# Attention with two MoE layers on one core: plain fp32 scores of two heads side by side

## The chip, the cores and the metric

The kernel runs on one core of one Trainium2 chip. The metric is the device time of one execution in microseconds (us). The engines are named as in the profile: PE is TensorE (PEld its weight loads), DVE VectorE, ACT ScalarE, POOL GpSimd, SP the queue that issues the DMAs.

## The reference

Attention over 4 batches and 8 heads (S = 576, D = 64) with a memory term, then two gated MoE layers on 2304 tokens; all in fp32:

```python
def _attn_ref(q, k, v, M_prev, z_prev, beta):
    scores = scale * np.matmul(q, k.transpose(0, 1, 3, 2))
    scores = np.where(causal, -1000000000.0, scores)
    a = np.exp(scores - scores.max(-1, keepdims=True))
    a /= a.sum(-1, keepdims=True) + 1e-09
    local = np.matmul(a, v)
    q_p = phi(q)                      # where(x > 0, x, exp(x) - 1) + 1
    mem_out = (q_p @ M_prev) / ((q_p @ z_prev)[..., None] + 1e-06)
    g = 1.0 / (1.0 + np.exp(-beta))
    return g * mem_out + (1 - g) * local
# x = attention output, (2304, 512); d_ff = 1536
x = (sigmoid(x @ w_gate) * (x @ w_val)) @ w_out
x = ((x @ w_a) * (x @ w_b)) @ w_out2
```

## The kernel before

Attention runs over 16 pairs of heads (`p`), four to a batch. The 576 rows of a head lie in five blocks of queries, the first of 64 rows, the others of 128, so that block `i` sees 128 i + 64 keys (64, 192, 320, 448, 576: 1600 key columns a head). The blocks are worked in two sets, `X_` = 0, 2, 3 and `Y_` = 1, 4.

For a pair, `load_rows` brings queries and keys in. `cut_q` cuts the queries into a rounded part (VectorE) and the rest (GpSimd), both of type fp32r; the keys are loaded twice. `turn` and `turn4` transpose them on TensorE into PSUM tiles `tp`, five blocks for each head and for each of the two; `put` scales the queries on VectorE, rounds the keys on ScalarE and takes the rest on VectorE. The 128 rows of a turned tile are the two parts of one head. `scores` multiplies: two fp32r products for a block and head, against the rounded keys and against the rest. `expo` adds the mask and takes the row extreme on VectorE (line 244), then the exponential on ScalarE. `turn_w` transposes the weights in three groups (A, B, C) and `evac` copies them to SBUF, all on ScalarE (`EDVE` is empty). `phi1` and `phi2` make the memory term, `sums` the denominators; `turn_mix` and `turn_r` transpose them. `pv` multiplies with the values: plain fp32 products, head 0 in output partitions 0 to 63 and head 1 in 64 to 127. `pv` of set X_ comes one iteration after its pair, that of Y_ at the start of the second iteration after.

Into this the first MoE layer is woven for three of the batches (`moe_a`): 48 steps a batch, each of three fp32r products of 512 columns (`mm3`, lines 490 to 492), four steps to a group that adds up in one PSUM bank. `Ms()` places one step (twelve of them in an iteration); a batch's steps begin when its four pairs are finished. At a group's end the bank is read by `gcopy` (VectorE), by `gat`, which goes through `gate` (line 568, VectorE), or by `fin`. `fill` places pieces of the preparation of the MoE weights (`w_stream`), on VectorE, ScalarE, GpSimd and by DMA. After the last pair the second stage begins with the products of `gv`.

PSUM has eight banks: two for `sc`, two for `sd` (both for scores; for the first four pairs alone, then `psm`, two banks for the MoE groups, has their place), four for `tp`. Instructions are written in the order of the iteration; a planner with a model of the times sets the order on each engine and holds an instruction back where its buffer isn't free.

Of the kernel before, what the change touches and what calls it, by code (L numbers as in the profile page):

```python
# [19 lines left out]
def kernel(  # L20
# [17 lines left out]
    P = 128  # L38
# [30 lines left out]
    pst = rctx.enter_context(tc.tile_pool(name="pst", bufs=4, space=bass.MemoryType.PSUM))  # L69
    pctx = ExitStack()  # L70
    psc = pctx.enter_context(
        tc.tile_pool(name="psc", bufs=1, space=bass.MemoryType.PSUM, side="right")
# [15 lines left out]
    ident_r = at.tile([P, P], F32R, name="ident_r", bufs=1)  # L88
    scs = [psa.tile([P, 1024], F32, tag="sc", name="sc"), psc.tile([P, 1024], F32, tag="sd", name="sd")]
# [67 lines left out]
    def cut_q(p):  # L157

        t = at.tile([P, NB, 2, 2, D], F32R, tag="qc", name="qc", bufs=1)
        vec.tensor_copy(out=t[:, :, :, 0], in_=st["qn", p])  # L160
        pool.tensor_tensor(
            out=t[:, :, :, 1], in0=st["qn", p], in1=t[:, :, :, 0].bitcast(F32), op=ALU.subtract
        )
        st["qc", p] = t

    def put(p, e, key, src, a, z):
        if key == "q":
            if a == 0:
                st["q", p, e] = at.tile([P, S], F32R, tag="qt", name="qt")
            vec.tensor_scalar(  # L170
                out=st["q", p, e][:, a:z], in0=src, scalar1=-1.0 / D ** 0.5, scalar2=None,
                op0=ALU.mult,
            )
            return
        if a == 0:
            st["k", p, e] = [at.tile([P, S], F32R, tag=x, name=x) for x in ("kh", "kl")]
        kh, kl = st["k", p, e]
        act.activation(out=kh[:, a:z], in_=src, func=AF.Copy)
        vec.tensor_tensor(
            out=kl[:, a:z], in0=src, in1=kh[:, a:z].bitcast(F32), op=ALU.subtract  # L180
        )

    def turn1(out, p, e, key, i):
        if key == "q":
            pe.transpose(
                out=out.bitcast(F32R), in_=st["qc", p][:, i, e].rearrange("p r d -> p (r d)"),
                identity=ident_r,
            )
        else:
            pe.transpose(  # L190
                out=out, in_=st["kn", p][:, i, e].rearrange("p r d -> p (r d)"), identity=ident
            )

    def turn(p, e, key):
        t = tp()
        for i, c in C03.items():
            turn1(t[:, c:c + P], p, e, key, i)
        put(p, e, key, t[:, 0:CUT], 0, CUT)

    def turn4(p, e):  # L200
        t = tp()
        for c, key in enumerate("kq"):
            turn1(t[:, c * P:(c + 1) * P], p, e, key, 4)
        for c, key in enumerate("kq"):
            put(p, e, key, t[:, c * P:(c + 1) * P], CUT, S)

    def sc_of(p, blocks):

        return scs[blocks is Y_ and p < NPAIR]

    def scores(p, e, blocks):
        sc = sc_of(p, blocks)
        qs, ks = st["q", p, e], st["k", p, e]
# [16 lines left out]
    def expo(p, e, blocks):  # L230
        if blocks is X_:
            st["mx", p, e] = at.tile([P, NB], F32, tag="mx", name="mx")
        sc = sc_of(p, blocks)
# [275 lines left out]
    def moe_a(b):  # L509
# [31 lines left out]
        def outp(u, c, f):  # L541
            if c == 0 and f == 0:
                mo[:] = [bank() for _ in H2]
            o = (2 * u + f) * P
            mm3(mo[f], ws[0, c, 2], slice(o, o + P), *gs[c], c == 0, c == MA - 1)

        def fin(u):
            io = pairs()
            vec.tensor_copy(out=io[:, 0], in_=mo[0])
            act.activation(out=io[:, 1], in_=mo[1], func=AF.Copy)  # L550
            nc.sync.dma_start(out=x2d[b][:, 2 * u:2 * u + 2], in_=io)
# [8 lines left out]
        for u in H2:  # L560
            for c in range(MA):
                for f in H2:
                    last = f and c == MA - 1
                    yield b, (0, c, 2), partial(outp, u, c, f), partial(fin, u) if last else None
# [14 lines left out]
    def start():  # L579
        make_identity(nc, ident)  # L580
        act.activation(out=ident_r, in_=ident, func=AF.Copy)
# [143 lines left out]
    EDVE = ""  # L725
    if True:
# [82 lines left out]
        cut_q(0)  # L809
        for e in H2:  # L810
            turn(0, e, "k")
            turn(0, e, "q")
            turn4(0, e)
        for p in range(NP + 2):
            new = p < NP
            nx = p + 1 if p + 1 < NP else None
            old = p - 1 if 0 < p <= NP else None
            last = p - 2 if p >= 2 else None
            if p == NPAIR:
                pctx.close()  # L820
                mctx = ExitStack()
                psm = mctx.enter_context(
                    tc.tile_pool(name="psm", bufs=2, space=bass.MemoryType.PSUM, side="right")
                )
# [4 lines left out]
            if new:  # L829
                scores(p, 0, X_)  # L830
                expo(p, 0, X_)
            Ms()
            if last is not None:
                pv(last, Y_)
            Ms()
            if old is not None:
                turn_w(old, 1, "B")
                turn_w(old, 1, "C")
            Ms()
            fill(p)  # L840

            if new:
                scores(p, 0, Y_)
                expo(p, 0, Y_)
            if old is not None:
                sums(old)
            Ms()
            if new:
# [3 lines left out]
                turn_w(p, 0, "A")  # L852
            if nx:
                cut_q(nx)
# [3 lines left out]
            if new:  # L858
                scores(p, 1, X_)
                expo(p, 1, X_)  # L860
            if nx:
                load_z(nx)
            Ms()
            if nx:
                turn(nx, 0, "k")
                turn(nx, 0, "q")
            Ms()
            if new:
                turn_w(p, 0, "B")
                turn_w(p, 0, "C")  # L870
            if nx:
                turn4(nx, 0)
            Ms()
            if old is not None:
                for name in "01Y":
                    turn_mix(old, name)
            fill(p)

            if new:
                scores(p, 1, Y_)  # L880
                expo(p, 1, Y_)
                phi2(p)
            Ms()
# [6 lines left out]
            if nx:  # L890
                turn(nx, 1, "k")
                turn(nx, 1, "q")
                turn4(nx, 1)
            if new:
                turn_w(p, 1, "A")
            Ms()
# [104 lines left out]
```

## Time and profile before

| | |
|---|---|
| median of 3 runs | 1172.28 us (1172.09 to 1174.34) |
| profiled execution | 1174.15 us, its span 1172.3 us |
| busy share of the span | PE 97%, PEld 80%, DVE 48%, ACT 41%, POOL 29% |
| attention with the woven first layer | to 359.37 us of the span |
| DMA | 89.67 MB, mean 76 GB/s |

Busy time of PE is the union of records whose ends are modelled, so a full PE can still hold short pauses. A plain fp32 product is two records on PE, an fp32r product or a transposition is one. A line can be that of a helper: 151 is every copy through `rnd`, 490 to 492 every `mm3`.

### The profile page before, as it was taken

To read this page: it belongs to the slowest core of one execution; us is meant where nothing else is said; L and a number is where in the kernel's file an instruction comes from. 1 tells how busy PE (TensorE), PEld (TensorE's weight loads), DVE (VectorE), ACT (ScalarE), POOL (GpSimd) and SP (SyncE) were. 2 spreads that over 40 slices of the span, in tenths; PEclk is the share of its full clock that TensorE was granted. 3 is DMA by queue.
4 is the path that set the end of the run, shared out by engine and by line. 5 is a ranking of instruction groups with operands and counts; after the bars stand their busy time and mean duration, and the time that the engine had idled before them with its cause. 6 is when DMAs were issued, how large, how long until landed. Compare 5 with 4: busy or idle time off the path is not lost.

```text
span 1172.3 us, 16189 instructions
## 1 busy us (share of the span) xinstructions
PE 1136.2 (97%) x6088; PEld 932.6 (80%) x6088; DVE 563.3 (48%) x1233; ACT 479.8 (41%) x1042; POOL 340.5 (29%) x330
## 2 busy tenths in 40 slices
PE   6889889999999999999999999999999999999998
PEld 5667678788777778998888888878888888888897
DVE  6898978565545995137621587851100200200111
ACT  5978767867853444134312234422111211211221
POOL 5786777463420112111111111111111111111111
PEclk9989989999999999999999999999999999999999
DMA  7454446243112443024420345311000200100010
GB/s 174 111 148 108 129 104 172 58 95 114 48 50 89 134 126 107 34 64 134 126 90 18 109 125 160 110 54 36 37 1 1 72 1 1 59 1 1 5 37 18
DMA packets 130814, 89.67 MB, mean 76 GB/s; under 512 B 90416, under 2 KB 118064, under 8 KB 129840
## 3 DMA queue, kind: packets, MB, share of 16 engines
q1 hardware_dynamic: 130736, 88.63, 26.2%
q8 instruction: 48, 0.79, 0.3%
q14 instruction: 30, 0.25, 0.1%
HBM read 71.31 MB, written 17.30 MB: 76 GB/s over the span
## 4 chain that ended last, share of the span: by engine, by line
PE 59%; DVE 5%; DMA 3%; issue 1%; POOL 0%; ACT 0%; POOLq 0%; DVEq 0%; ACTq 0%
PE gv L492 13%; PE gv L491 13%; PE gv L490 13%; PE mo L687 4%; PE mo L686 4%; PE mo L685 4%; PE mo L491 3%; PE mo L492 3%; PE mo L490 3%; DMA st<-in_moe_w_gate_dram 2%; DMA st<-in_moe_w_out_dram 1%; DVE w L459 1%; DVE wl L446 1%; DVE wt L417 1%; DVE st L456 1%; DVE wl L420 1%
## 5 line engine op out<-in xcount | busy, mean ns | idle before, releaser
L574 POOL TENSOR_TENSOR gl<-sg,gh 128x512 fp32r<-128x512 f32 (+1 forms) x120 | 143.6, 1197 | 698.0 <-ACT gh L151 670.9
L492 PE MATMUL gv<-xs,w 128*128 128x512 f32 (+1 forms) x864 | 318.3, 368 | 0.0
L490 PE MATMUL gv<-xs,w 128*128 128x512 f32 (+1 forms) x864 | 318.3, 368 | 0.0
L491 PE MATMUL gv<-xs,w 128*128 128x512 f32 (+1 forms) x864 | 318.2, 368 | 0.0
L568 DVE TENSOR_TENSOR sg<-gv,sg 128x512 f32<-128x512 f32 (+1 forms) x108 | 68.0, 630 | 417.6 <-PE gv L492 413.0
L490 PEld LDWEIGHTS gv<-xs,w 128*128 128x128 f32 x864 | 162.7, 188 | 29.5
L491 PEld LDWEIGHTS gv<-xs,w 128*128 128x128 f32 x864 | 162.8, 188 | 29.4
L492 PEld LDWEIGHTS gv<-xs,w 128*128 128x128 f32 x864 | 162.7, 188 | 28.7
L151 ACT ACTIVATE gh<-sg 128x512 fp32r<-128x512 f32 (+1 forms) x120 | 70.6, 588 | 208.8 <-DVE sg L568 208.5
L655 ACT ACTIVATE sg<-gv 128x512 f32<-128x512 f32 (+1 forms) x108 | 59.0, 547 | 220.6 <-PE gv L492 216.7
L249 ACT ACTIVATE s<-s,mx 128x320 f32<-128x320 f32 (+3 forms) x128 | 78.0, 611 | 25.2 <-DVE mx L244 24.4
L687 PE MATMUL mo<-w,gl 128*128 128x512 f32 x216 | 85.1, 394 | 0.6 <-POOL gl L574 0.5
L686 PE MATMUL mo<-w,gh 128*128 128x512 f32 x216 | 84.8, 393 | 0.0
L685 PE MATMUL mo<-w,gh 128*128 128x512 f32 x216 | 84.8, 392 | 0.0
L151 ACT ACTIVATE aw<-tp 128x512 f32<-128x512 f32 (+1 forms) x144 | 70.6, 508 | 27.7 <-PE tp L330 21.4
L418 ACT ACTIVATE wt<-wt,rebias 128x512 int32<-128x512 int32 x72 | 51.6, 721 | 66.1 <-DVE wt L417 66.0
L491 PE MATMUL mo<-gl,w 128*128 128x512 f32 (+1 forms) x192 | 70.9, 369 | 3.8 <-POOL gl L574 3.6
L244 DVE CUSTOM_DVE_ANT_0 s<-sc,mask 64x64 f32<-64x64 f32 (+4 forms) x144 | 62.2, 470 | 19.9 <-PE sc L219 19.8
L490 PE MATMUL mo<-gh,w 128*128 128x512 f32 (+1 forms) x192 | 70.4, 366 | 0.0
L492 PE MATMUL mo<-gh,w 128*128 128x512 f32 (+1 forms) x192 | 70.2, 366 | 0.0
L219 PE MATMUL sc<-kh,qt 128*64 128x64 f32 (+1 forms) x168 | 54.1, 344 | 4.4 <-ACT s L249 1.9
L455 ACT ACTIVATE w<-wt 128x512 fp32r<-128x512 f32 x57 | 36.1, 633 | 48.2 <-DVE wt L452 48.0
(111 smaller groups left out, 1840.4 us busy)
## 6 DMA issues: line engine op xcount, KB each, us to landing
st<-in_moe_w_out_dram SPq DMA_DIRECT2D x24, 512.0 KB, 3.5
kn<-in_k_dram SPq DMA_DIRECT2D x64, 128.0 KB, 2.8
st<-in_moe_w_gate_dram SPq DMA_DIRECT2D x12, 512.0 KB, 4.2
st<-in_moe_w_val_dram SPq DMA_DIRECT2D x12, 512.0 KB, 3.6
st<-in_moe_w_a_dram SPq DMA_DIRECT2D x12, 512.0 KB, 3.6
st<-in_moe_w_b_dram SPq DMA_DIRECT2D x12, 512.0 KB, 3.7
xd<-x SPq DMA_DIRECT2D x16, 288.0 KB, 2.7
qn<-in_q_dram SPq DMA_DIRECT2D x32, 128.0 KB, 2.7
```

The lines of the kernel that those rows point to most:

```text
L151: act.activation(out=out, in_=src, func=AF.Copy)
L244: st["pace"] = vec.tensor_tensor_reduce(out=s, in0=sc[0:m, SC0[i]:SC0[i] + w], in1=mask[0:m, c:c + w], scale=1.0, scalar=BIG, op0=ALU.add, ...
L249: act.activation(out=o, in_=s, func=AF.Exp, scale=-1.0, bias=mx[0:m, i:i + 1], accum_out=sm[0:m, i:i + 1],)
L490: pe.matmul(o, lhsT=w[:, 0, ws_], rhs=xh, start=first, stop=False, skip_group_check=True)
L491: pe.matmul(o, lhsT=w[:, 0, ws_], rhs=xl, start=False, stop=False, skip_group_check=True)
L492: pe.matmul(o, lhsT=w[:, 1, ws_], rhs=xh, start=False, stop=last, skip_group_check=True)
L568: st["gate"] = vec.tensor_tensor(out=s[:, 0:n], in0=vps[:, 0:n], in1=s[:, 0:n], op=ALU.mult)
L574: pool.tensor_tensor(out=gl[:, 0:n], in0=s[:, 0:n], in1=gh[:, 0:n].bitcast(F32), op=ALU.subtract)
L655: act.activation(out=s[:, 0:n], in_=tg[:, 0:n], func=AF.Copy if layer else AF.Sigmoid)
L685: pe.matmul(mo[f], lhsT=gh[:, t], rhs=w[:, 0], start=first, stop=False)
L686: pe.matmul(mo[f], lhsT=gh[:, t], rhs=w[:, 1], start=False, stop=False)
L687: pe.matmul(mo[f], lhsT=gl[:, t], rhs=w[:, 0], start=False, stop=c == NCH - 1)
```

## The change

Queries and keys are turned uncut, both heads in one tile: the 128 rows of a turned tile are head 0 (0 to 63) and head 1 (64 to 127). So a pair has ten turns in place of twenty, and `cut_q`, the second load of the keys and the split of the turned keys go. The scores are plain fp32 products over 64 rows, for a block first head 0 and then head 1, each into its own two banks `sc0` and `sc1`. An iteration has two score phases (X_ and Y_, both heads) and not four. `pv` of Y_ follows `pv` of X_ in the iteration after the pair; the loop has 17 iterations, before 18. The MoE steps stay twelve in an iteration, at other places. PSUM: four banks for scores, three for `tp`, one for MoE groups; the output products of a MoE batch go one bank after the other. The minimum in `phi1` moves from GpSimd to VectorE, the evacuation of group C from ScalarE to VectorE. Buffers of the exponentials go from two to three, those of the groups B and C from three to two.

```diff
-    pst = rctx.enter_context(tc.tile_pool(name="pst", bufs=4, space=bass.MemoryType.PSUM))
+    pst = rctx.enter_context(tc.tile_pool(name="pst", bufs=3, space=bass.MemoryType.PSUM))
+    psm = mctx.enter_context(
+        tc.tile_pool(name="psm", bufs=1, space=bass.MemoryType.PSUM, side="right")
...
-    scs = [psa.tile([P, 1024], F32, tag="sc", name="sc"), psc.tile([P, 1024], F32, tag="sd", name="sd")]
+    scs = [psa.tile([P, 1024], F32, tag=f"sc{e}", name="sc") for e in H2]
...
-        st["kn", p] = at.tile([P, NB, 2, 2, D], F32, tag="kn", name="kn", bufs=1)
-        for r in H2:
-            load_rows(st["kn", p][:, :, :, r], k, p)
+        st["kn", p] = at.tile([P, NB, 2, D], F32, tag="kn", name="kn", bufs=2)
+        load_rows(st["kn", p], k, p)
...
-    def cut_q(p):
...
+    def put(p, key, src, a, z):
+        if a == 0:
+            st[key, p] = at.tile([P, S], F32, tag=f"{key}t", name=f"{key}t")
+        t = st[key, p][:, a:z]
         if key == "q":
             vec.tensor_scalar(
+                out=t, in0=src, scalar1=-1.0 / D ** 0.5, scalar2=None, op0=ALU.mult
             )
         else:
+            act.activation(out=t, in_=src, func=AF.Copy)
+
+    def turn1(out, p, key, i):
+        src = st[f"{key}n", p][:, i].rearrange("p h d -> p (h d)")
+        pe.transpose(out=out, in_=src, identity=ident)
...
+    def scores(p, blocks):
         for i in blocks:
             w, m = width(i), rows(i)
             r0 = max(P * i - 64, 0)
             for a, z in [(0, w)] if i < 4 else [(0, ZX), (ZX, w)]:
-                for s in H2:
+                for e in H2:
+                    r = slice(64 * e, 64 * e + 64)
                     st["anchor"] = pe.matmul(
-                        sc[0:m, SC0[i] + a:SC0[i] + z], lhsT=qs[:, r0:r0 + m], rhs=ks[s][:, a:z],
-                        start=(s == 0), stop=(s == 1),
+                        scs[e][0:m, SC0[i] + a:SC0[i] + z], lhsT=st["q", p][r, r0:r0 + m],
+                        rhs=st["k", p][r, a:z], start=True, stop=True,
                     )
...
-        both = at.tile([P, wa + wb], F32, tag=f"s{blocks[-1]}", name="s")
+        both = at.tile([P, wa + wb], F32, tag=f"s{blocks[-1]}", name="s", bufs=3)
...
-        pool.tensor_scalar(out=e, in0=qn, scalar1=0.0, scalar2=None, op0=ALU.min)
+        vec.tensor_scalar(out=e, in0=qn, scalar1=0.0, scalar2=None, op0=ALU.min)
...
-        st["a", p, e, name] = evac("aw" + name, t, len(NAMES[name]) * P, 3, name in EDVE)
+        st["a", p, e, name] = evac("aw" + name, t, len(NAMES[name]) * P, 3 if name == "A" else 2, name in EDVE)
...
+        def outp(f, c):
+            if c == 0:
+                mo[:] = [bank()]
+            mm3(mo[0], ws[0, c, 2], slice(f * P, f * P + P), *gs[c], c == 0, c == MA - 1)
...
-    EDVE = ""
+    EDVE = "C"
...
+        for p in range(NP + 1):
...
             if new:
+                scores(p, X_)
+                for e in H2:
+                    expo(p, e, X_)
             if old is not None:
+                for e in H2:
+                    turn_w(old, e, "B")
+            Ms()
             if old is not None:
+                for e in H2:
+                    turn_w(old, e, "C")
+                sums(old)
+            Ms(2)
             fill(p)
             if new:
                 phi1(p)
                 if p:
                     load_v(p)
             if nx:
+                load_z(nx)
+                for key in "kq":
+                    turn(nx, key)
             Ms(2)
             fill(p)
             if new:
+                scores(p, Y_)
+                for e in H2:
+                    expo(p, e, Y_)
             Ms()
             if old is not None:
                 for name in "01Y":
                     turn_mix(old, name)
+            Ms()
+            if nx:
+                turn4(nx)
             fill(p)
             if new:
+                for e in H2:
+                    turn_w(p, e, "A")
                 phi2(p)
+            Ms(2)
             if old is not None:
                 room(old)
                 turn_r(old, X_)
                 turn_r(old, Y_)
                 Ms()
                 pv(old, X_)
+                pv(old, Y_)
+            Ms(2)
             fill(p)
```

## Rows read from the trace of the kernel before

**Rows 1.** The page, busy tenths of each engine in 40 slices of the span.

```profile
PE   6889889999999999999999999999999999999998
...
DVE  6898978565545995137621587851100200200111
```

**Rows 2.** Four stretches: length, busy (xcount) of PE, PEld, DVE, ACT, POOL; PEclk, DMA, GB/s.

```profile
0.00:10.84 10.84, 3.56 (x18) 2.89 (x19) 3.77 (x11) 3.79 (x8) 6.54 (x11) 1.00 0.59 132
10.84:159.65 148.81, 129.97 (x907) 103.75 (x907) 132.11 (x364) 118.01 (x316) 110.64 (x109) 0.95 0.52 133
159.65:359.37 199.72, 199.40 (x1351) 159.07 (x1350) 121.49 (x348) 134.89 (x339) 95.34 (x104) 0.99 0.33 86
359.37:450.00 90.63, 86.99 (x374) 69.52 (x373) 78.38 (x134) 40.75 (x64) 13.94 (x10) 1.00 0.42 128
```

**Rows 3.** All engines in order of time, the start: us, length, what [idle before].

```profile
7.05 1.53 POOL L161 TENSOR_TENSOR qc<-qn,qc 128x640 fp32r<-128x640 f32 x1
...
8.63 0.57 PEld L185 LDWEIGHTS tp<-ident_r,qc 128*128 128x128 f32 x4 [0.41 <-POOL qc L161]
```

**Rows 4.** VectorE's groups by line, 10 to 360 us: busy us, mean ns | idle.

```profile
L170 DVE TENSOR_SCALAR qt<-tp 128x448 fp32r<-128x448 f32 x32 | 19.7, 616 | 7.2 <-PE tp L185 7.2
L179 DVE TENSOR_TENSOR kl<-tp,kh 128x448 fp32r<-128x448 f32 x32 | 19.6, 612 | 8.3 <-ACT kh L178 8.1
...
L179 DVE TENSOR_TENSOR kl<-tp,kh 128x128 fp32r<-128x128 f32 x32 | 9.0, 281 | 1.6 <-ACT kh L178 1.5
L160 DVE CAST qc<-qn 128x640 fp32r<-128x640 f32 x15 | 8.9, 593 | 0.0
L170 DVE TENSOR_SCALAR qt<-tp 128x128 fp32r<-128x128 f32 x32 | 8.8, 277 | 0.0
```

**Rows 5.** TensorE in order of time, 200 to 222 us (pairs 8 and 9).

```profile
200.09 0.60 PE L190 MATMUL tp<-ident,kn 128*128 128x128 f32 x4
200.45 0.54 PE L185 MATMUL tp<-ident_r,qc 128*128 128x128 f32 x4
200.82 0.47 PE L490 MATMUL m<-xs,w 128*128 128x512 f32 x1
...
201.71 0.34 PE L219 MATMUL sc<-kh,qt 128*128 128x192 f32 x1
...
202.55 0.40 PE L490 MATMUL m<-xs,w 128*128 128x512 f32 x1
...
204.71 1.65 PE L343 MATMUL tp<-ident,mix 64*128 64x64 f32 x10
206.12 0.27 PE L219 MATMUL sc<-kh,qt 128*64 128x64 f32 x1
...
207.16 0.64 PE L360 MATMUL tp<-ident,rt 64*128 64x64 f32 x3
...
210.85 1.25 PE L385 MATMUL tp<-aw,vn 128*64 128x256 f32 x12
212.04 0.65 PE L190 MATMUL tp<-ident,kn 128*128 128x128 f32 x4
```

**Rows 6.** Line 385, 210.2 to 212.1 us: ns min/median/max, starts, forms.

```profile
L385 PE MATMUL tp<-aw,vn x12: 272/379/379, 210.9 to 211.8; 128*64 128x256 f32 x8, 128*64 128x128 f32 x4
```

**Rows 7.** In order of time, records that begin before 211.0 us.

```profile
210.85 0.39 PE L385 MATMUL tp<-aw,vn 128*64 128x256 f32 x2
```

**Rows 8.** In order of time: ends of two MoE groups (135 to 141, 314 to 317 us).

```profile
135.55 0.39 PE L492 MATMUL m<-xs,w 128*128 128x512 f32 x1
...
139.79 0.68 DVE L568 TENSOR_TENSOR sg<-m,sg 128x512 f32<-128x512 f32 x1
...
314.05 0.39 PE L491 MATMUL m<-xs,w 128*128 128x512 f32 x1
...
314.28 0.39 PE L492 MATMUL m<-xs,w 128*128 128x512 f32 x1
...
314.81 0.69 DVE L568 TENSOR_TENSOR sg<-m,sg 128x512 f32<-128x512 f32 x1
```

More of the change, by code (lines that the diff above doesn't have):

```diff
@@ L68 @@
     psa = rctx.enter_context(tc.tile_pool(name="psa", bufs=1, space=bass.MemoryType.PSUM))
-    pst = rctx.enter_context(tc.tile_pool(name="pst", bufs=4, space=bass.MemoryType.PSUM))
-    pctx = ExitStack()
-    psc = pctx.enter_context(
-        tc.tile_pool(name="psc", bufs=1, space=bass.MemoryType.PSUM, side="right")
+    pst = rctx.enter_context(tc.tile_pool(name="pst", bufs=3, space=bass.MemoryType.PSUM))
+    mctx = ExitStack()
+    psm = mctx.enter_context(
+        tc.tile_pool(name="psm", bufs=1, space=bass.MemoryType.PSUM, side="right")
     )
@@ L87 @@
     rebias = const.tile([P, 1], F32, name="rebias")
-    ident_r = at.tile([P, P], F32R, name="ident_r", bufs=1)
-    scs = [psa.tile([P, 1024], F32, tag="sc", name="sc"), psc.tile([P, 1024], F32, tag="sd", name="sd")]
+    scs = [psa.tile([P, 1024], F32, tag=f"sc{e}", name="sc") for e in H2]
     sms = [at.tile([P, NB, 2], F32, name=f"sm{i}", bufs=1) for i in H2]
@@ L154, in tp @@
         return pst.tile([P, 512], F32, tag="tp", name="tp")
-    def cut_q(p):
[L159 to L166, printed above, removed]
+    def put(p, key, src, a, z):
+        if a == 0:
+            st[key, p] = at.tile([P, S], F32, tag=f"{key}t", name=f"{key}t")
+        t = st[key, p][:, a:z]
@@ L167, in put @@
         if key == "q":
-            if a == 0:
-                st["q", p, e] = at.tile([P, S], F32R, tag="qt", name="qt")
             vec.tensor_scalar(
[L171 to L187, printed above, removed]
-            )
-        else:
-            pe.transpose(
-                out=out, in_=st["kn", p][:, i, e].rearrange("p r d -> p (r d)"), identity=ident
-            )
@@ L194, in turn @@
-    def turn(p, e, key):
+                out=t, in0=src, scalar1=-1.0 / D ** 0.5, scalar2=None, op0=ALU.mult
+            )
+        else:
+            act.activation(out=t, in_=src, func=AF.Copy)
+    def turn1(out, p, key, i):
+        src = st[f"{key}n", p][:, i].rearrange("p h d -> p (h d)")
+        pe.transpose(out=out, in_=src, identity=ident)
+    def turn(p, key):
         t = tp()
         for i, c in C03.items():
-            turn1(t[:, c:c + P], p, e, key, i)
-        put(p, e, key, t[:, 0:CUT], 0, CUT)
@@ L200, in turn4 @@
-    def turn4(p, e):
+            turn1(t[:, c:c + P], p, key, i)
+        put(p, key, t[:, 0:CUT], 0, CUT)
+    def turn4(p):
         t = tp()
         for c, key in enumerate("kq"):
-            turn1(t[:, c * P:(c + 1) * P], p, e, key, 4)
+            turn1(t[:, c * P:(c + 1) * P], p, key, 4)
         for c, key in enumerate("kq"):
[L205 to L213, printed above, removed]
+            put(p, key, t[:, c * P:(c + 1) * P], CUT, S)
@@ L232, in expo @@
             st["mx", p, e] = at.tile([P, NB], F32, tag="mx", name="mx")
-        sc = sc_of(p, blocks)
+        sc = scs[e]
         mx, sm = st["mx", p, e], sms[p % 2][:, :, e]
         wa, wb = width(blocks[-2]), width(blocks[-1])
-        both = at.tile([P, wa + wb], F32, tag=f"s{blocks[-1]}", name="s")
+        both = at.tile([P, wa + wb], F32, tag=f"s{blocks[-1]}", name="s", bufs=3)
         st["w", p, e, blocks[-2]], st["w", p, e, blocks[-1]] = both[:, 0:wa], both[:, wa:wa + wb]
@@ L539, in gat, with fin @@
                 finished.append(b)
[L541 to L551, printed above, removed]
+        def outp(f, c):
+            if c == 0:
+                mo[:] = [bank()]
+            mm3(mo[0], ws[0, c, 2], slice(f * P, f * P + P), *gs[c], c == 0, c == MA - 1)
+        def fin(f):
+            if f % 2 == 0:
+                sg["io"] = pairs()
+            io = sg["io"]
+            if f % 2:
+                act.activation(out=io[:, 1], in_=mo[0], func=AF.Copy)
+                nc.sync.dma_start(out=x2d[b][:, f - 1:f + 1], in_=io)
+            else:
+                vec.tensor_copy(out=io[:, 0], in_=mo[0])
         for kind, then in ((0, gcopy), (1, gat)):
@@ L559, in moe_a @@
                     )
-        for u in H2:
+        for f in range(KD):
             for c in range(MA):
-                for f in H2:
-                    last = f and c == MA - 1
-                    yield b, (0, c, 2), partial(outp, u, c, f), partial(fin, u) if last else None
+                yield (
+                    b, (0, c, 2), partial(outp, f, c), partial(fin, f) if c == MA - 1 else None
+                )
     def gate(vps, s, n, tag="g"):
@@ L580, in start @@
         make_identity(nc, ident)
-        act.activation(out=ident_r, in_=ident, func=AF.Copy)
         vec.memset(rebias, -896.0 * 2 ** 23)
@@ L808 @@
         load_v(0)
[L809 to L814, printed above, removed]
+        for key in "kq":
+            turn(0, key)
+        turn4(0)
+        for p in range(NP + 1):
             new = p < NP
             nx = p + 1 if p + 1 < NP else None
[L817 to L824, printed above, removed]
+            old = p - 1 if p else None
             if nx:
@@ L829 @@
             if new:
[L830 to L834, printed above, removed]
+                scores(p, X_)
+                for e in H2:
+                    expo(p, e, X_)
+            if old is not None:
+                for e in H2:
+                    turn_w(old, e, "B")
             Ms()
             if old is not None:
-                turn_w(old, 1, "B")
-                turn_w(old, 1, "C")
-            Ms()
+                for e in H2:
+                    turn_w(old, e, "C")
+                sums(old)
+            Ms(2)
             fill(p)
[L842 to L847, printed above, removed]
             if new:
@@ L851 @@
                     load_v(p)
-                turn_w(p, 0, "A")
             if nx:
-                cut_q(nx)
+                load_z(nx)
+                for key in "kq":
+                    turn(nx, key)
             Ms(2)
@@ L858 @@
             if new:
[L859 to L872, printed above, removed]
+                scores(p, Y_)
+                for e in H2:
+                    expo(p, e, Y_)
             Ms()
@@ L876 @@
                     turn_mix(old, name)
+            Ms()
+            if nx:
+                turn4(nx)
             fill(p)
             if new:
-                scores(p, 1, Y_)
-                expo(p, 1, Y_)
+                for e in H2:
+                    turn_w(p, e, "A")
                 phi2(p)
-            Ms()
+            Ms(2)
             if old is not None:
@@ L889 @@
                 pv(old, X_)
[L890 to L896, printed above, removed]
+                pv(old, Y_)
+            Ms(2)
             fill(p)
```

## The prediction

> **What bounds the kernel now.** I read the busy slices first, then the time of each engine in four stretches, then the costs by line, then TensorE's queue in order of time. The change touches the attention stage and the first MoE layer that is woven into it, so the end of that stage is the number that matters: the first `gv` product of the next stage follows the last woven product at 359.37 us, and nothing that the later stages do is changed. In the slices, 29.3 us each, VectorE is about as full as TensorE for the first seven and half full for the next six [rows 1]. The stretches [rows 2] make that sharp. From 10.84 to 159.65 us (pairs 0 to 7) VectorE is busy 132.11 of 148.81 us, ScalarE 118 and GpSimd 111, TensorE has gaps: VectorE sets the pace, with two engines close behind. From 159.65 to 359.37 us (pairs 8 to 15 and the tail) TensorE is busy 199.40 of 199.72 us and VectorE 121: here only TensorE counts. Before 10.84 us nothing scores yet. So each part of the change has three prices, one for each stretch.
>
> After 359.37 us the next stage is paced by VectorE (78 of 90.63 us) preparing weights. That work starts when attention has given up its space, so a stage that ends earlier moves the rest earlier, whole.
>
> **The start.** Today a pair needs queries cut into two parts (`cut_q`: VectorE, then 1.53 us on GpSimd) and two copies of the keys. The first query turn waits for GpSimd's cut until 8.63 us [rows 3], and the first scores start at 10.84. After the change there is no cut and half the key loads. I take 2.5 us off: GpSimd's 1.53 us plus some 0.9 us for one head's eight turns less ahead of the first score [rows 5]. Bounds: 0 (if the query load itself is late) and 4 us (both heads ready at once).
>
> **Pairs 0 to 7, VectorE's price.** Removed for each pair [rows 4]: the cast of the queries 0.59 us; four cut-off parts of the keys, 2 x 0.612 + 2 x 0.281 = 1.79 us; one of the two scalings of the queries, 0.616 + 0.277 = 0.89 us. Sum 3.27 us. Added: the minimum over 128x640 that leaves GpSimd; no row has it on VectorE, its bounds are the cast of the same size, 0.59, and the scaling stretched from 448 to 640 columns, 0.88; I take 0.65, near the cast, since both go from SBUF to SBUF. And the two "C" evacuations of 384 columns that leave ScalarE: 0.69 us for 512 from PSUM [rows 8] gives 0.52 each, 1.04. Net -1.58 us a pair, 12.6 us over eight. ScalarE and GpSimd lose more than that each, so neither takes over. What can eat it: the four score phases of a pair become two, so that VectorE has fewer other things in hand while it waits for scores. I take 10 us; bounds 0 (the pace is a chain of waits and not VectorE's load) and 14.
>
> **Pairs 8 to 15, TensorE's price.** The clearest rows are TensorE's queue in order of time [rows 5]. Turns of keys and queries: four and four run from 200.09 to 200.82 us, 0.09 us each; a pair has twenty, of which ten go, 0.9 us. Seven pairs are still turned in this stretch: -6.3 us.
>
> Scores: one head's blocks 1 and 4 run from 201.71 to 202.55 us, its blocks 0, 2 and 3 from 206.12 to 207.16: 1.88 us a head, 3.76 a pair. The new form is a plain fp32 product, and the value products show its price. Each is two records in the trace; a record of 256 columns lasts 0.379 us, one of 128 columns 0.272 [rows 6], so 0.84 ns a column for each. Twelve records with 2560 columns in all would take 2.15 us one after another; they took 1.19 us, from 210.85 to 212.04 [rows 5], and the first two lie on top of each other, 0.39 us for both [rows 7]. So two heads on two halves of the array run at once. There the halves are output columns, in the new scores they are contraction rows; no row shows that kind. If it pairs too, a pair of heads needs 1600 columns x 2 records x 0.84 ns = 2.7 us; if not, 5.4 us. I take pairing, since the value products show two tiles of the array working independently.
>
> To this comes the cost of changing the tile size. Ten turns of `mix`, two of them with 64 rows, take 1.41 us from 204.71 to 206.12 where ten of the full size would take 0.9: 0.5 us for four changes, 0.12 each. The new scores have five changes a pair (into block 0, out of it, out of that phase, in and out of the other), 0.6 us, so 3.3 us a pair and -0.5 against today: -4 us over eight pairs. (The Trainium skill, "TensorEngine Tiling (Array Packing)", section "Key Properties", says that changing the tiling mode drains TensorE. That speaks against this form and agrees with the 0.12 us; had the trace shown no such cost, the saving would be 1.0 us a pair and the sum 4 to 5 us lower.)
>
> Woven MoE steps: twelve a pair before and after, three products of 0.23 us each [rows 8]. A batch of 48 steps can start when its four pairs are finished, which today is after the first quarter of the second iteration behind, and after the change at the end of the one before. So three steps of the first batch move out of this stretch: 9 x 0.23 = -2.1 us.
>
> **What it costs: the banks.** Both heads now hold score space at once. The turns keep three banks of four (they have 16 tiles a pair instead of 19), and the MoE steps one of two. A group of twelve products then has to be evacuated before the next group's first product. In TensorE's stretch the way from the last product's start to the end of its evacuation is 314.28 to 315.50 us, 1.2 us; in VectorE's stretch 135.55 to 140.47, 4.9 us, since the evacuation queues behind other VectorE work [rows 8]. With two banks this hides: TensorE shows no gap. With one, behind the waiting product stand the next pair's scores and turns in TensorE's queue, and behind those VectorE's reductions. The full price is 1.2 - 0.23 = 1.0 us for each of the 24 groups in TensorE's stretch; zero if turns or value products always stand between two groups. There are 11 to 12 us of attention work in each iteration and three groups, so most can be covered; I take a third of the full price, +8 us, bounds 0 and 24. For three instead of four turn banks, and for the last pair's value products which now stand directly ahead of the next stage with little behind them to hide their evacuation, +2 us (0 to 4).
>
> **The sum.** -2.5 - 10 - 6.3 - 4 - 2.1 + 8 + 2 = -14.9 us. The profiled execution took 1174.15 us, 1.85 us over its span of 1172.3 and 1.87 us over the median of the runs, 1172.28; so 1159.3 us by it and about 1157 us by the median.
>
> **Rivals.** (a) *The single MoE bank decides.* The gains come to 24.9 us and the other costs to 2; over all 36 groups the change breaks even when a group costs 0.6 us on average. At the full 1.0 us in TensorE's stretch and about 1 us for each of the twelve in VectorE's, the cost is 36 instead of 8: 1157 + 28 = 1185 us. For it: VectorE's stretch shows evacuations far behind, and TensorE executes its queue in order. Against it: there is other TensorE work to put between.
> (b) *The row halves do not pair.* 5.4 + 0.6 = 6.0 us a pair instead of 3.3, 2.7 x 8 = 22 us more, and some 3 us more in pairs 5 to 7, where TensorE has the woven steps already: 1182 us. That is the case in which the change doesn't do what it says.
> (c) *VectorE's load isn't the pace in pairs 0 to 7.* Its waits there are short, but if the chain from scores to exponentials sets the pace, the 10 us go: 1167 us.
> (d) *Everything hides.* No cost of banks and the upper bounds of the gains: -4 - 14 - 6.3 - 4 - 2.1, 1142 us.
>
> **How the numbers follow.** Forecast 0.55 (1145 to 1166 us), (a) at or past break-even 0.18, (b) 0.10, (c) 0.09, (d) 0.08. The predicted time is the forecast's, 1157 us. The range runs from (d) to just short of (a) and (b), 1141 to 1181 us: it leaves out the worse halves of both and a little below. About 0.2% (2.3 us) is what a measurement of this kernel can tell from no change. Faster: forecast, (c) and (d), 0.72, less a little for sums that end near zero, 0.70; within 0.2%: the mild end of (a), 0.07; slower: the rest of (a) and (b), 0.23.
>
> **What would show it.** Right: `gv` starts near 345 us instead of 359; VectorE stays the fullest engine up to about 147 us; the four score records of one block lie two on two, and a pair's scores take 3 to 3.5 us of TensorE's queue; gaps of TensorE ahead of the woven products sum to under 10 us. Wrong: score records of the two heads strictly one after the other (b); waits of TensorE on the MoE evacuations (the copy to `sg`, the gate, the output copy) of 20 us and more (a); iterations of pairs 0 to 7 as long as before with more idle time of VectorE (c).

## The result, and the profile after

The changed kernel takes 1188.03 us (median of four executions, 1184.85 to 1191.87) where the kernel before takes 1172.18 in the same comparison: 1.0134 of the time, 95% interval 1.0094 to 1.0174, so 15.9 us slower. The forecast was 1157.0, range 1141 to 1181. The profiled execution took 1191.87 us, its span 1190.0, 17.7 us more than the profiled one of before; the sums below are made between these two.

The page of the changed kernel, busy tenths in 40 slices of 29.75 us, answers to [rows 1]:

```profile
PE   7999999999999999999999999999999999999998
...
DVE  5779795554543898116730488861100200200111
PEclk8889899999999999999999999999999999999999
```

In four of the first five slices VectorE has become lighter, as meant (in the fourth it is fuller), and TensorE is fuller than before. By stretches (columns as in [rows 2]):

```profile
10.84:159.65 148.81, 139.52 (x782) 94.04 (x779) 114.66 (x318) 104.12 (x271) 80.00 (x89) 0.87 0.45 116
159.65:340.00 180.35, 178.99 (x1063) 127.13 (x1063) 102.50 (x296) 113.94 (x282) 67.95 (x84) 1.00 0.26 72
```

In the first stretch TensorE is busy 9.6 us longer than in [rows 2] and has run 125 records fewer. In the second it is full with 1063 records; the kernel before ran 1221 in the same 180.35 us:

```profile
159.65:340.00 180.35, 180.03 (x1221) 145.04 (x1221) 117.58 (x341) 129.97 (x328) 94.79 (x104) 0.98 0.35 91
```

The ten turns dropped explain some 70 of those 158 records. For the others a record takes longer on average (168 ns of busy time against 147): a full TensorE here is not a TensorE that does much.

The start of each pair's first reduction on VectorE (in time order, the one of 64x64 elements; set X_, the first head) gives the pace, in us of the span. "Last product" is the last woven one:

| | pair 0 | pair 8 | pair 15 | last product |
|---|---|---|---|---|
| before | 13.9 | 161.6 | 317.8 | 359.1 |
| after | 11.7 | 170.2 | 337.1 | 376.0 |
| `e1_side_by_side` | 12.1 | 174.7 | 334.9 | 375.6 |
| `e8c_shared_banks_only` | 11.8 | 159.1 | 321.3 | 362.0 |
| `e8b_shared_paired` | 11.9 | 155.3 | 306.2 | 345.3 |
| `b3_three_turn_banks_in_before` | 13.7 | 175.2 | 337.2 | 375.9 |

After: -2.2 at the start, +10.8 over pairs 0 to 7, +10.7 over pairs 8 to 14, -2.4 from there: +16.9 us at the last product. The next stage gives nothing back. Both profiled executions also have stretches at half the TensorE clock; how much of the +10.8 they can be is worked out in the last section.

Now the scores, in time order on TensorE. Set Y_ of a pair, blocks 1 and 4, then the last two blocks of an X_:

```profile
268.54 1.56 PE L190 MATMUL sc<-kt,qt 64*128 64x192 f32 x6
270.03 0.44 PE L331 MATMUL tp<-ident,rt 128*128 128x128 f32 x2
...
278.83 1.56 PE L190 MATMUL sc<-kt,qt 64*128 64x192 f32 x6
280.32 0.50 PE L461 MATMUL m<-gh,w 128*128 128x512 f32 x1
...
288.31 0.66 PE L301 MATMUL tp<-ident,s 128*128 128x128 f32 x4
288.90 1.56 PE L190 MATMUL sc<-kt,qt 64*128 64x320 f32 x8
290.39 0.50 PE L461 MATMUL m<-xs,w 128*128 128x512 f32 x1
```

The group at 288.90 is both heads on blocks 2 and 3: two times 768 key columns in 1.49 us, up to the next product. The groups at 268.54 and 278.83 are one head each, 768 columns (192 + 256 + 320) in 1.49 us. So two heads side by side take the time of one, the row halves do pair; and the two heads of a Y_ were not side by side but 10 us apart. The code writes them next to each other; the planner, which sets the order, put the second head later. Over the whole stage 156 of the 384 score records run two by two in this trace; that is 39 of the 96 pairs of products (the expectations below say 40). Summing, for each score record, the time to the start of the next record on TensorE: 0.59 us per 1000 columns of a record where they stand side by side, 1.07 where a head is alone.

### The profile page after: what moved, and what is told of

It reads as the page before. It is cut to its first block, busy times and chain, and to the rows that moved or that the text cites. A ratio compares the mean times of both kernels' runs of the same rounds, so it can differ in the third digit from the quotient of the medians.

```text
span 1190.0 us, 15630 instructions
## 1 busy us (share of the span) xinstructions
PE 1164.3 (98%) x5928; PEld 918.9 (77%) x5928; DVE 542.2 (46%) x1169; ACT 460.0 (39%) x977; POOL 285.8 (24%) x298
## 4 chain that ended last, share of the span: by engine, by line
PE 57%; DVE 6%; DMA 3%; issue 1%; POOL 0%; ACT 0%; POOLq 0%; DVEq 0%; ACTq 0%
PE gv L462 13%; PE gv L461 13%; PE gv L463 13%; PE mo L660 4%; PE mo L659 4%; PE mo L658 4%; PE mo L462 3%; PE mo L463 3%; PE mo L461 3%; DMA st<-in_moe_w_out_dram 2%; DVE w L430 1%; DVE wl L417 1%; DVE wt L388 1%; DVE st L427 1%; DVE wt L423 1%
## 5 line engine op out<-in xcount | busy, mean ns | idle before, releaser
L190 PE MATMUL sc<-kt,qt 64*128 64x320 f32 (+4 forms) x384 | 91.7, 434 | 2.4 <-DVE mx L215 2.2
L215 DVE CUSTOM_DVE_ANT_0 s<-sc,mask 64x64 f32<-64x64 f32 (+4 forms) x160 | 70.3, 479 | 31.7 <-PE sc L190 24.9
L220 ACT ACTIVATE s<-s,mx 128x192 f32<-128x192 f32 (+3 forms) x128 | 77.8, 610 | 17.5 <-DVE mx L215 16.0
L148 ACT ACTIVATE aw<-tp 128x512 f32<-128x512 f32 (+2 forms) x112 | 56.3, 515 | 53.1 <-PE tp L301 23.1
L190 PEld LDWEIGHTS sc<-kt,qt 64*128 64x128 f32 (+1 forms) x384 | 50.6, 188 | 24.2 <-issue 9.8
```

The source lines that it names most:

```text
L148: act.activation(out=out, in_=src, func=AF.Copy)
L190: st["anchor"] = pe.matmul(scs[e][0:m, SC0[i] + a:SC0[i] + z], lhsT=st["q", p][r, r0:r0 + m], rhs=st["k", p][r, a:z], start=True, stop=True,)
L215: st["pace"] = vec.tensor_tensor_reduce(out=s, in0=sc[0:m, SC0[i]:SC0[i] + w], in1=mask[0:m, c:c + w], scale=1.0, scalar=BIG, op0=ALU.add, ...
L220: act.activation(out=o, in_=s, func=AF.Exp, scale=-1.0, bias=mx[0:m, i:i + 1], accum_out=sm[0:m, i:i + 1],)
```

## The experiments

The theories at first, with the letters of the expectations: the parted scores in TensorE's queue (A), the single MoE bank and the three turn banks (B), the lower granted clock (C). Later ones: a loop of buffers from one iteration to the next (D), too few turn banks whatever holds them (E), the banks as the whole loss (F), banks and buffers without the scores (G). "Turn banks" are those of the tiles `tp`. Changes against the kernel before are taken from the ratio, those between runs from the medians.

**1. The heads put side by side.** Head 1's product is written first and head 0's is tied to it.

```diff
-                for e in H2:
+                for e in (1, 0):
                     r = slice(64 * e, 64 * e + 64)
-                    st["anchor"] = pe.matmul(
+                    with tc.issue_after(st["anchor"].ins) if e == 0 else ExitStack():
+                        st["anchor"] = pe.matmul(
...
```

> The changed kernel with one thing more: of the two heads' products of a block, head 1's is written first and head 0's is held behind it in TensorE's queue, so that 91 of the 96 pairs of products stand next to each other (in the changed kernel 40). Theory A (the loss is score products that run one head at a time: 228 of 384 records alone, 1.07 ns a column, 156 in pairs, 0.59): the scores' share of TensorE's queue falls from 90.6 us to 60 to 65, and the kernel comes to 1158 to 1170 us. Theory B (the single MoE bank and the three turn banks): TensorE still waits, 1182 to 1192 us. Theory C (the lower granted clock of the first 130 us): the same stretches at half clock, 1178 to 1190 us.

Measured: 1187.30 us, 1.0132 of before [1.0115, 1.0149]; no change from the changed kernel. Yet 91 of 96 pairs now stand side by side, and the scores' share of TensorE's queue (start to next start) falls from 90.6 to 65.5 us. The stretches of this kernel show where the 25 us went:

```profile
10.84:159.65 148.81, 125.30 (x770) 84.30 (x768) 113.83 (x312) 101.25 (x266) 80.55 (x88) 0.87 0.43 115
159.65:340.00 180.35, 171.30 (x1072) 120.07 (x1074) 103.39 (x302) 113.74 (x290) 67.95 (x86) 0.99 0.27 73
```

TensorE is busy 14.2 and 7.7 us less than after the change, and the last woven product comes 0.3 us earlier. Waits have taken the place of the slow scores, so there is a second bound of about the same length. The clock isn't enough for that: over the first 400 us half clock lasts 44.4 us here and 37.5 after the change, which is 3.5 us of time at most.

**2. The heads held apart.** All of head 0's products of a set, then all of head 1's.

```diff
-        for i in blocks:
+        for e in H2:
+            for i in blocks:
...
```

> The changed kernel with all products of head 0 of a phase written ahead of head 1's, so that no two stand side by side. Theory A: 102400 record columns at 1.07 ns are 110 us in place of 90.6, so 1200 to 1210 us. Theories B and C: nothing they rest on is touched, 1183 to 1192 us.

Measured: 1221.53 us (two executions), 1.0429 [1.040, 1.0458]. The scores' share goes from 90.6 to 124.4 us, +33.8, and the kernel from 1188.0 to 1221.5, +33.5. In this direction TensorE's queue is the bound and every microsecond counts (the clock doesn't bring it: half clock lasts 17.1 us over the first 400, after the change 37.5); in the other (run 1) none does. Alone throughout, a head costs 1.21 us per 1000 columns, more than the 1.07 that the expectation took.

**3. Two MoE banks, two turn banks,** on top of run 1.

```diff
-    pst = rctx.enter_context(tc.tile_pool(name="pst", bufs=3, space=bass.MemoryType.PSUM))
+    pst = rctx.enter_context(tc.tile_pool(name="pst", bufs=2, space=bass.MemoryType.PSUM))
...
-        tc.tile_pool(name="psm", bufs=1, space=bass.MemoryType.PSUM, side="right")
+        tc.tile_pool(name="psm", bufs=2, space=bass.MemoryType.PSUM, side="right")
```

> As the side-by-side kernel, but two banks for the MoE groups and two (not three) for the turns. All 96 pairs of products stand side by side. Theory A: the waits ahead of the MoE products in the changed kernel are about 5 us, so at most that is won and something is lost to the turns: within 6 us of the side-by-side kernel, either way. Theory B: 10 us and more below the side-by-side kernel.

Measured: 1265.41 us, 1.0806 [1.079, 1.0823], 78 us more than run 1. Up to 27 us of that can be the clock: over the first 400 us half clock lasts 99.0 us here, 44.4 in run 1. TensorE's largest waits, up to 430 us (waiting line, who released it: us in total, times, longest):

```profile
PE tp L302 <- ACT aw L148: 14.6, 4, 5.5
PE tp L332 <- ACT x L337: 9.2, 13, 2.0
PE tp L351 <- ACT x L337: 6.6, 14, 0.5
```

All three are tiles `tp`, which wait for a turn bank to be read out. Giving up a turn bank for a second MoE bank is far dearer than it is worth, which neither theory had.

**4. The banks of the change, in the kernel before**, where nothing else is changed: one MoE bank (with the output products one bank after the other, as in the change), three turn banks, and both.

```diff
-                    tc.tile_pool(name="psm", bufs=2, space=bass.MemoryType.PSUM, side="right")
+                    tc.tile_pool(name="psm", bufs=1, space=bass.MemoryType.PSUM, side="right")
...
```

> The kernel before with one change alone: one PSUM bank for the MoE groups in place of two (and the output products one bank after the other, as in the changed kernel). My prediction's term: +8 us, bounds 0 and 24. Theory A: 0 to 6 us slower, since the planner puts other work between. Theory B: 10 to 24 us slower.

Measured: 1181.60 us, 1.0088 [1.0073, 1.0103], +10 us.

```diff
-    pst = rctx.enter_context(tc.tile_pool(name="pst", bufs=4, space=bass.MemoryType.PSUM))
+    pst = rctx.enter_context(tc.tile_pool(name="pst", bufs=3, space=bass.MemoryType.PSUM))
```

> The kernel before with one change alone: three turn banks in place of four. My prediction's term was +2 us (0 to 4). Theory E (three are too few): 10 us and more slower. Theory D: 0 to 6 us slower, since the turn banks hurt only where one is held.

Measured: 1195.15 us, 1.0197 [1.0168, 1.0226], +23 us. Its stretches, and the waits of TensorE in the first of them:

```profile
10.84:159.65 148.81, 123.26 (x829) 95.92 (x828) 124.69 (x344) 110.53 (x292) 103.14 (x103) 0.94 0.48 124
159.65:340.00 180.35, 171.29 (x1162) 136.41 (x1161) 113.25 (x330) 125.69 (x314) 90.25 (x98) 0.99 0.37 95
```

```profile
PE tp L330 <- DVE qt L170: 7.6, 9, 1.5
PE tp L190 <- DVE x L391: 4.4, 2, 2.2
```

TensorE has about the same gap in the second stretch as in run 1, 171.29 against 171.30 us busy, and again turns wait for a bank (the first line is 3.3 us in the kernel before).

> The kernel before with the bank budget of the changed kernel and nothing else of it: three turn banks and one MoE bank (two banks stay unused). Theory F (the time is lost with the banks, and the change's gains are about what I forecast): the two prices measured alone, 22 and 10 us, add up, 1195 to 1210 us, slower than the changed kernel itself. If they overlap, 1190 to 1197 us. Theory A (the score products that run alone are the loss): not above 1185 us.

Measured: 1192.56 us, 1.0172 [1.0142, 1.0202], +20 us. The two do not add up; why was not tested.

**5. More buffers**, on top of run 1: four for the turned weights of group A; four for the exponentials; both (there with one buffer for the keys in place of two, for space). In run 1's trace an evacuation of A waits for the value products of the pair before to give up its buffer, and holds a turn bank meanwhile:

```profile
271.13 1.25 PE L357 MATMUL tp<-aw,vn 128*64 128x256 f32 x12
272.26 0.60 ACT L148 ACTIVATE aw<-tp 128x512 f32<-128x512 f32 x1 [0.87 <-PE tp L357]
```

```diff
-        st["a", p, e, name] = evac(..., 3 if name == "A" else 2, name in EDVE)
+        st["a", p, e, name] = evac(..., 4 if name == "A" else 2, name in EDVE)
```

> The side-by-side kernel with four buffers for the evacuated group A in place of three. There the second A evacuation of an iteration waits for the value products of the pair before (at 272.26 us, 0.87 us idle until them), with its transposes done some 4 us earlier, so that it holds one of the three turn banks all that time. Theory D (with the scores side by side the time is set by a loop of buffers from one iteration to the next, not by TensorE's work): this is a link of the loop; the 25.5 us that the turns of the denominators take fall to about 13, the kernel to 1172 to 1182 us. Theory E (three turn banks are too few whatever holds them): within 4 us of 1187.

> The side-by-side kernel with four buffers for the exponentials' inputs in place of three. There head 1's reduction for set X_ starts only when group B of the pair before is transposed (277.25 us, right behind 276.72), which itself comes after the value products of the pair before that. Theory D: the other link of the loop; VectorE's idle time ahead of it goes, 1172 to 1182 us. Theory E: within 4 us of 1187.

> Both at once: four buffers for group A and four for the exponentials' inputs, side by side scores; to make room the keys have one buffer instead of two. Theory D: both links are gone and TensorE's work decides again, that is 25 us less of scores than in the changed kernel: 1158 to 1170 us. Theory E: within 5 us of 1187.

Measured: 1183.42 us (1.009 [1.0068, 1.0112]), 1184.04 (1.0106 [1.008, 1.0132]) and 1178.39 (1.0047 [1.0026, 1.0068]): 4, 3 and 9 us less than run 1. The first two are as E expected, the third lies between D and E. The waits for buffers are real, but they are not the main part.

**6. Four banks shared.** The MoE groups take their bank from the turns' pool. Still eight banks in all; only the rule who may use which is gone. First on top of the third kernel of 5, then alone on the changed kernel (scores as the planner puts them), then the first without the tie of run 1.

```diff
-    pst = rctx.enter_context(tc.tile_pool(name="pst", bufs=3, space=bass.MemoryType.PSUM))
+    pst = rctx.enter_context(tc.tile_pool(name="pst", bufs=4, space=bass.MemoryType.PSUM))
...
-            return psm.tile([P, 512], F32, tag="m", name="m")
+            return pst.tile([P, 512], F32, tag="tp", name="m")
```

> The kernel with side-by-side scores and four A and four exponential buffers, in which the MoE groups take their bank from the turns' pool, now of four: until the fifth pair, when no MoE step is woven in, the turns have four banks again, later they share. Theory F: what the banks cost comes back in part, all of it in the first five pairs: 1160 to 1172 us, and the first reduction of pair 4 about 8 us earlier than with three and one. Theory D (the loop of buffers): nothing left to win there, 1175 to 1180 us.

> The changed kernel with that one thing: MoE groups and turns share four banks (in place of three and one); scores and buffers as in the changed kernel, so the planner is again free to part the two heads' products. Theory F: 1174 to 1184 us. Theory A: 1184 to 1192 us, since as many products run alone as before.

> The changed kernel with the shared four banks and the four A and exponential buffers (keys one), but the planner free to part the two heads' products: 59 of 96 pairs of products stand together, 91 or so in the kernel with everything (1167 us). Theory A in its rest (parted products cost time once the banks don't bind): TensorE streams some 37 pairs of products more one head at a time, 10 to 15 us, so 1174 to 1182 us. Theory G (banks and buffers are all; scores don't matter): 1165 to 1170 us.

Measured: 1167.14 us (0.9948 [0.993, 0.9966]); 1182.55 (1.0083 [1.0057, 1.011]); 1174.59 (1.0021 [0.9999, 1.0043]). Sharing alone is worth 5.5 us by the medians; the two intervals overlap, but at like granted clock the gain is 7 to 8 us (1177.68 against 1184.85 and 1185.47 us at 0.991, 1183.62 against 1191.87 at 0.983). On the third kernel of 5 it is worth 11 us, of which 7.5 go again when the tie of run 1 is taken out.

**7. Shared banks and heads side by side, nothing else.**

> The changed kernel with the shared four banks and the products side by side, but three A and three exponential buffers (keys two) as in the changed kernel. Theory D in its rest (the held bank costs as much as in the side-by-side kernels with three and one banks, 9 us): 1172 to 1180 us. Theory G without the buffers: 1165 to 1170 us.

Measured: 1162.39 us (1161.62 to 1165.21), 0.992 [0.9896, 0.9944]. It is the fastest of all and beats both kernels, the one before by 0.8%, and lies below both ranges that were expected. Its stretches:

```profile
10.84:159.65 148.81, 128.96 (x869) 87.98 (x869) 126.33 (x348) 111.68 (x298) 92.01 (x100) 0.95 0.48 125
159.65:340.00 180.35, 179.30 (x1170) 130.37 (x1165) 99.17 (x296) 115.11 (x286) 61.96 (x82) 1.00 0.26 73
```

TensorE is full again in the second stretch, and now with 1170 records instead of 1063. The two edits in one table, in us:

| | scores as planned | side by side |
|---|---|---|
| three turn banks and one MoE bank | 1188.0 | 1187.3 |
| four shared | 1182.6 | 1162.4 |

Neither edit alone gives more than 5.5 us, both give 25.6. That is how two bounds of like length look: TensorE's stream with the parted scores, and the way of the tiles through too few banks. The clock makes the contrast look larger than it is. The executions of the four kernels have mean granted clocks of 0.988 and 0.984 in the first row, 0.987 and 0.992 in the second. Between executions of like clock side by side alone gives 6 us (at 0.983) or 2 (0.986 against 0.987), sharing alone 7 to 8 (0.983 and 0.991), both 22 to 23 (0.991 against 0.992).

In pairs 8 to 14 of the profiled executions there is hardly any half clock (6.8 us in `e8c_shared_banks_only`, 3.9 before, else none). From first reduction to first reduction they take, in us, before 156.2:

| pairs 8 to 14 | scores as planned | side by side |
|---|---|---|
| three turn banks and one MoE bank | 166.9 | 160.2 |
| four shared | 162.2 | 150.9 |

Here each edit alone does gain, 6.7 and 4.7 us, and both 16.0.

With the extra buffers of 5 the median is 5 us higher (1167.1 against 1162.4); at a clock of 0.988 it is 2 us (1167.1 to 1167.4 against 1165.21). Which of the buffers (that kernel also has one less for the keys) wasn't separated.

**8. The two moves to VectorE, alone in the kernel before**: the minimum and the evacuation of group C.

```diff
-        pool.tensor_scalar(out=e, in0=qn, scalar1=0.0, scalar2=None, op0=ALU.min)
+        vec.tensor_scalar(out=e, in0=qn, scalar1=0.0, scalar2=None, op0=ALU.min)
...
-    EDVE = ""
+    EDVE = "C"
```

> The kernel before with the two moves to VectorE alone: the minimum of the memory term (from GpSimd) and the evacuation of group C (from ScalarE). They put 0.65 + 1.04 us on VectorE for each pair. If VectorE's load sets the pace in pairs 0 to 7, as I took it, that is up to 13 us: 1178 to 1187 us. If a chain of waits sets it, 1168 to 1176 us.

Measured: 1167.84 us over ten executions, 0.9959 [0.9944, 0.9974], 5 us faster, of which 2 can be the clock (0.995 on average, before 0.993). The engine that was said to set the pace got more work, and the kernel did not become slower. The profiled execution, at 1172.25 us the slowest of the ten, shows both sides: from the first reduction of pair 0 to that of pair 5 it takes 7.1 us more than before, where five times 1.69 is 8.5; from there to pair 8 it takes 5.2 less, and from pair 9 on its reductions are 2 to 4 us earlier than before. So the load does tell in the first pairs, and more than that comes back later. That it is the freed ScalarE and GpSimd that bring it fits, but wasn't tested apart.

## Why the prediction was wrong

*The start, -2.5:* right, the first reduction is at 11.68 us, before at 13.9: -2.2.

*Turns of keys and queries, -6.3 over seven pairs (0.9 a pair):* right as time of TensorE. Their share of its queue over the whole stage falls from 39.0 to 24.2 us, 14.8 for 16 pairs, 0.92 each. As time of the kernel it doesn't show, since the scores' share grew by 23.6 us.

*Two moves to VectorE, 0.65 and 1.04 us a pair:* the minimum costs less than its lower bound, the two evacuations 1.10:

```profile
L146 DVE COPY aw<-tp 128x384 f32<-128x384 f32 x32 | 16.5, 549 | 2.5 <-PE tp L301 2.5
...
L233 DVE TENSOR_SCALAR e<-qn 128x640 f32<-128x640 f32 x16 | 7.8, 486 | 1.8 <-DMA qn<-in_q_dram 1.8
```

*Pairs 0 to 7, -10 by VectorE's load:* wrong in sign, +10.8. VectorE's work did fall (124.3 us busy from the first reduction of pair 0 to that of pair 8, before 130.7), and TensorE's rose (149.1, before 129.5), so that VectorE was no longer the fullest engine there, which had been a sign of being right. The step that failed is "VectorE sets the pace": it was read from a busy share of 89%. Run 8 put 13.5 us of forecast work on VectorE in these pairs, and they took 1.9 us more; only the first five pairs were slower by most of the price. With scores and banks mended (run 7) pairs 0 to 7 take 143.4 us, before 147.8: -4.4, not -10. That the 10 us go is rival (c). What made the +10.8 is not settled: the parted scores and the turn banks act here too (three turn banks alone, run 4: +13.8 in these pairs), but up to 10.4 us of it can be half clock.

*Scores, 3.3 us a pair if they pair:* the hardware part was right. Side by side (run 7) the scores' share is 60.1 us, 3.8 a pair, against 67.0, 4.2, before: a gain of 0.4 where 0.5 was forecast. In the changed kernel it is 90.6, 5.7 a pair, near rival (b)'s 6.0, though not for (b)'s reason. The step that failed is an unsaid one: that products written next to each other run next to each other. The queue is ordered by a planner, and the text itself says of it that it holds back an instruction whose buffer isn't free; that it can part two heads was not weighed.

*Woven steps, -2.1:* 106 woven products start ahead of the first reduction of pair 8, before 100. Six have moved, 1.4 us, where nine were forecast.

*The single MoE bank, +8 (0 to 24):* right in size where it stands alone, +10 (run 4). In the changed kernel TensorE's idle time ahead of the woven products, up to 380 us, shows this most (what ended it: us, times):

```profile
  DVE sg L542: 5.0, 7
  DVE sg L502: 3.4, 2
```

These count the weight loads and the products both; of the products alone the trace has 3.8 us. Rival (a) needed 36.

*Three turn banks, +2 (0 to 4):* the term that was most mis-sized. Alone in the kernel before, three banks cost 23 us. The argument, "16 tiles a pair instead of 19", counts tiles; it leaves out how long a tile holds its bank, which is up to the engine that empties it and to the buffer that this engine waits for (271.13 to 272.26 us in 5). The trace of before had the sign: even with four banks, turns wait there for VectorE to read a turn bank (3.3 us, three times, in the first stretch). (The Trainium skill, "TensorEngine Tiling (Array Packing)", section "PSUM Bottleneck", says that tiling speeds up TensorE but not the evacuation of PSUM, which may then be the bottleneck. Runs 1 and 7 fit that: with three and one banks the paired scores are worth 0.7 us by the medians, with four shared ones 20.2. That it is the evacuation no run shows by itself; what was varied is the number of banks and who may use them.)

*A sign that was none:* `gv` near 345 us. In the changed kernel `gv` starts at 354.15 us, before 359.37, and yet the stage ends later: the planner has begun `gv` ahead of the last woven products, the last of which starts at 375.98 us. The mark is the last woven product.

*The sum.* Run 7 has what the forecast counted on, heads that pair and banks that decide less, and takes 1162.4 us, 9.4 less than the kernel before in its comparison; the forecast was 14.9 less, with 10 us of costs for the banks in it. What four shared banks still cost is not known, so gains of 24.9 us were not seen. The two conditions of the gains, products that stay together and banks that don't hold up the tiles, were both missed. What part of the 15.9 us each has can't be told: by the medians either alone is enough to hold the time within 5.5 us of where it is, and some 3 to 4 us go with the clock (last section). The new order of the iteration and the fewer buffers of groups B and C are in every run on the changed kernel and were not tried apart.

## What to carry to other kernels

When a change takes buffers that rotate, ask of each how long it is held and by whom, not how many tiles pass through it; a price is had by taking one such buffer from the unchanged kernel. Where an order is planned and not written, two instructions that gain only side by side have to be tied together. And mend the suspects together as well as one by one: with two bounds of like length each single repair can look nearly worthless.

## What the runs showed of the hardware

Two heads on the two row halves of the array run at once in plain fp32: 1.49 us for both where one alone takes 1.49.

The granted clock fell for longer in the changed kernel. In its profile (columns as in [rows 2]):

```profile
13.60:20.30 6.70, 6.23 (x35) 4.18 (x34) 3.27 (x13) 5.94 (x20) 1.04 (x4) 1.00 1.03 272
20.34:37.40 17.06, 17.06 (x55) 11.26 (x55) 11.45 (x38) 11.26 (x32) 7.56 (x12) 0.50 0.27 58
37.50:57.80 20.30, 18.87 (x128) 12.27 (x124) 17.03 (x52) 15.21 (x46) 12.20 (x16) 1.00 0.49 128
```

For 17 us the clock is 1.2 and not 2.4 GHz, between two stretches at full clock. Ahead of it TensorE was busy 6.23 of 6.70 us. Later, from 159.65 to 340 us, it is busy 178.99 of 180.35 us and the clock stands at 1.00. The kernel before is at full clock between 21.00 and 37.40 us:

```profile
21.00:37.40 16.40, 12.48 (x91) 10.23 (x93) 14.74 (x54) 14.28 (x44) 12.19 (x15) 1.00 0.49 116
```

Over the first 400 us half clock lasts 20.5 us before, 37.5 after, 44.4 in run 1, 13.7 in run 7. After the change all of it lies in pairs 0 to 7, where before has 16.6; half clock can at most double the time of TensorE's work, so up to 10.4 of the 10.8 us lost there can be this. Of the 10.7 us lost in pairs 8 to 14 none is: the changed kernel is at full clock there.

The executions tell how much of the whole it is. Those of the changed kernel stand at 1184.85 and 1185.47 us with a mean clock of 0.991, 1190.59 with 0.986 and 1191.87 with 0.983; in `e8c_shared_banks_only` time and clock go together in the same way (1177.68 us at 0.991, 1187.33 at 0.982), in run 1 hardly (1186 us at 0.983, 1188.55 at 0.987). The kernel before takes 1171.48 to 1174.96 us in its six executions at 0.991. So at that clock the change still costs 10 to 14 us, 12.4 on average, in place of 15.9. What brought the clock down stays open: no run changed the clock alone.
